# Tying a block's small copy behind its turned rows, an early all-ones matrix, and a sign moved into an eviction

## The chip, the cores and the metric

The kernel runs on one core of a Trainium2 chip. The metric is the device time of one execution in microseconds (us); lower is better. The engines are TensorE (PE in the rows, its weight loads PEld), VectorE (DVE), ScalarE (ACT), GpSimd (POOL) and SyncE (SP, which here only issues DMAs).

## The reference

The input x has 8 sequences of 2496 tokens with 256 channels. Each sequence is filtered along the tokens in the frequency domain; the 19968 filtered tokens then go through a mixture of eight experts, one expert for each token.

```
X = np.fft.rfft(x, axis=1)
y = np.fft.irfft(X * (filt_r + 1j * filt_i), n=S, axis=1)
...
logits = x @ w_gate + modality_bias[modality_id]
e_idx = np.argmax(logits, axis=1)
probs = np.exp(logits - max); probs /= probs.sum(-1)
...
h = np.maximum(x[mask] @ w1[e], 0.0)
out[mask] = gate_w[mask, None] * (h @ w2[e])
```

## The kernel before, in words

**Filter.** The transform of 2496 points is split into 48 x 52. Stage 1 (`stage1`, L194) multiplies by a 96x96 matrix and writes to a scratch tensor b1_d in DRAM. Stage 2 (`stage2`, L458) reads it back as tile `t` (L448), multiplies by `w2m` (L464), evicts `xf` (L477), multiplies by the filter tiles `g1` and `g2` on VectorE (L479, L480), multiplies by `a1m` and `a2m` into `pz` (L472, L473) and writes b2_d. Stage 3 (`stage3`, L491) reads b2_d, multiplies by `wbm`, and forms the gate's logits.

**Start-up.** The matrices are made on the chip in a part whose order is written out by hand (`manual_schedule`, L232 to L421). `a1m` and `a2m` come from transposing products with `perm`, evicted at L341: `a1m` on VectorE, `a2m` on ScalarE. The imaginary filter `g2` is loaded in two halves, of which the second is a copy of the first (L307, L308), and three VectorE instructions at L345 multiply it by a sign that depends on the partition alone (`sgn`). Much further on VectorE fills `ones_sq` (L376), with which a small matmul `mb_ps` (L409) spreads the gate's bias over the partitions. TensorE's `busy` matmuls (L824) have no use for the result; they are work put between the steps.

**Experts.** After a sequence's stage 3, `count` and `place` give each token a place in its expert's bin, and `scatter` (L596, an indirect DMA on the GpSimd queue, 20 for a sequence) writes the rows, each with its token number and gate, to `bins_d` in DRAM. `load` (L672) reads a block of 256 rows into tile `xs` (five buffers, L678, on the SP queue); it waits for the scatters that stand ahead of it in the program. `turn` (L688) copies the expert's weights (`w1`, L694), copies the token numbers and gates out of `xs` into `meta` (L700, eight buffers), transposes the rows on TensorE (`pT`, L704, one buffer) and copies the turned rows to `xT` (L705, VectorE). `up` (L710, matmuls `hps`, L715, eviction L720) needs `xT`; `down` (L722) makes `ops` (L728), scales it by the gate in `meta` into `osb` (L735) and writes the rows to the output with an indirect DMA on the GpSimd queue (`out_dram`, L737). A block takes 16 matmuls of each of L715 and L728; `down` of one block runs between the steps of `up` of the next. There are 79 blocks.

**Order.** Outside the part written by hand, a scheduler puts the instructions of each engine in order as the program is built; `tc.issue_after(x)` ties an instruction behind x. `behind` (L667) uses it for the weight copies and the loads. Nothing ties `meta`, whose only input is `xs`. On the chip each engine takes its instructions in that order.

Of the kernel before, what the change touches and what calls it, by code (L numbers as in the profile page):

```python
# [13 lines left out]
I32 = mybir.dt.int32  # L14
AF = mybir.ActivationFunctionType
# [5 lines left out]
P = 128  # L21
# [7 lines left out]
def kernel(  # L29
# [12 lines left out]
    nc = tc.nc  # L42
# [14 lines left out]
    NS = N1 // 2  # L57
    NTT = N2 // 2
    KA = 2 * N1
    KB = 2 * N2  # L60
# [10 lines left out]
    NI = BLK // P  # L71
# [4 lines left out]
    DW = D // 2  # L76
# [31 lines left out]
    a1m = fft_pool.tile([KB, NS, KB], BF16, name="a1m")  # L108
    a2m = fft_pool.tile([KB, NS, KB], BF16, name="a2m")
    g1 = fft_pool.tile([KB, NS, D], BF16, name="g1")  # L110
    g2 = fft_pool.tile([KB, NS, D], BF16, name="g2")
# [38 lines left out]
    def row_int(expr_ops, base, name):  # L150

        t = fft_pool.tile([P, 1], I, name=name + "_int")
        nc.vector.tensor_copy(t, base)
        for op, v in expr_ops:
            nc.vector.tensor_single_scalar(t, t, v, op=op)
        f = fft_pool.tile([P, 1], F32, name=name)
        nc.vector.tensor_copy(f, t)
        return f
# [3 lines left out]
    def col(name, fn):  # L162
        t = fft_pool.tile([P, 1], F32, name=name)
        fn(t)
        return t

    def ts(out, in_, s1, s2, op0=ALU.mult, op1=ALU.add):
        nc.vector.tensor_scalar(out, in_, scalar1=s1, scalar2=s2, op0=op0, op1=op1)
# [50 lines left out]
    ones_sq = const_pool.tile([P, P], F32)  # L219
# [12 lines left out]
    with tc.manual_schedule():  # L232
# [25 lines left out]
        nc.sync.dma_start(mb_sb, moe_modality_bias.rearrange("a e -> (a e)")[None, :])  # L258


        rows = row_int([], rows_i, "rows")
        bit0 = row_int([(ALU.bitwise_and, 1)], rows_i, "bit0")
        half = row_int([(ALU.arith_shift_right, 1)], rows_i, "half")
# [66 lines left out]
        sgn = col("sgn", lambda t: ts(t, x_hi, -2.0, 1.0))  # L330
        x_c0 = col("x_c0", lambda t: nc.vector.tensor_single_scalar(t, x_c, 0.0, op=ALU.is_equal))
        wt0 = col("wt0", lambda t: ts(t, x_c0, -0.5, 1.0))
        SPB = 4
        for s0 in range(0, NS, SPB):
            for src, dst in ((w2m, a1m), (w2x, a2m)):
                tp = pp.tile([P, EV * D], F32, tag="ps", name="tp")
                for i in range(SPB):
                    nc.tensor.matmul(tp[:KB, i * KB:(i + 1) * KB], lhsT=src[:, s0 + i, :], rhs=perm,
                                     start=True, stop=True)
                ev = nc.vector.tensor_copy if dst is a1m else nc.scalar.copy  # L340
                ev(dst[:, s0:s0 + SPB, :].rearrange("p s c -> p (s c)"), tp[:KB, 0:SPB * KB])  # L341
            if s0 == 0:
                nc.vector.tensor_scalar_mul(a1m[:, 0, :], a1m[:, 0, :], wt0[:KB])
        for ga, gb in ((1, 8), (8, 16), (16, NS)):
            nc.vector.tensor_scalar_mul(g2[:, ga:gb, :], g2[:, ga:gb, :], sgn[:KB])  # L345


        zs = col("zs", lambda t: nc.vector.tensor_single_scalar(t, quart, 0.0, op=ALU.is_equal))
# [24 lines left out]
        for b in range(3):  # L373
            mv = mrawc[:, b].rearrange("p g (t two) -> p g t two", two=2)
            nc.vector.tensor_copy(mids[KA:P, :, b:NYF:3], mv[KA:P, :, 3:4 * NYG:4, 0])
        nc.vector.memset(ones_sq, 1.0)  # L376

        eio_i = const_pool.tile([P, E], I32)
        nc.gpsimd.iota(eio_i, pattern=[[1, E]], base=0, channel_multiplier=0)
# [62 lines left out]
    ep = ctx.enter_context(tc.tile_pool(name="expert", bufs=2))  # L442
# [224 lines left out]
    def behind(what, n):  # L667

        m = marks[what]
        return tc.issue_after(m[-n]) if len(m) >= n else nullcontext()  # L670
# [17 lines left out]
    def turn(b):  # L688

        xh = b["xs"].bitcast(BF16)  # L690
        with behind("w1", 1):
            ej = nc.values_load(b["ej_i"], engines=(ET.DVE,), min_val=0, max_val=E - 1)
        b["w1"] = ep.tile([P, DC, F], BF16, tag="w1", name="w1")
        cp = nc.vector.tensor_copy(b["w1"].rearrange("p a f -> p (a f)"),  # L694
                              w1sb[:, ds(ej, 1)].rearrange("p o a f -> p (o a f)"))
        marks["w1"].append(cp.ins)
        b["xT"] = ep.tile([P, DC, NI, P], BF16, tag="xT", name="xT")

        b["meta"] = ep.tile([P, NI, 2], I32, tag="meta", bufs=8, name="meta")
        nc.vector.tensor_copy(b["meta"], b["xs"][:, :, DW:DW + 2])  # L700
        pT = op.tile([P, DC, NI, P], BF16, tag="tr")
        for dc in range(DC):
            for i in range(NI):
                nc.tensor.transpose(pT[:, dc, i, :], xh[:, i, dc * P:(dc + 1) * P], ident)  # L704
        nc.vector.tensor_copy(b["xT"], pT)  # L705
        b["hT"] = ep.tile([P, FT, NI * P], BF16, tag="hT", name="hT")

    FQ = 2
# [48 lines left out]
    class Experts:  # L757
# [26 lines left out]
        def begin(self, b):  # L784
            if b is not None:
                turn(b)
                self.fill()
# [144 lines left out]
```

## Time and profile before

| | us |
|---|---|
| median of 3 runs | 711.7 |
| lowest, highest | 709.67, 718.71 |
| profiled execution | 709.73 |
| its span, first to last instruction | 707.6 |
| TensorE busy in the span | 580.3 |
| VectorE, ScalarE, GpSimd busy | 369.9, 379.9, 365.8 |

The rows are of one profiled execution, 709.73 us, of which 2.1 us lie outside the span. Start times in rows count from the span's start. In rows of the timeline the bracket at the end is the idle time of the engine before the instruction, and what ended it. The span falls into a start-up (to about 180 us, when the first block of an expert is turned), a middle in which filter and experts are interleaved (to about 548 us), a stretch in which the last sequence's rows are scattered (to about 585 us), and an end in which only blocks are left.

### The profile page before, as it was taken

What the parts mean: (1) busy time and instruction counts of PE and PEld (TensorE: products, weight loads), DVE (VectorE), ACT (ScalarE), POOL (GpSimd) and SP (SyncE); (2) the same over time, 40 slices, a digit from 0 to 9 for tenths busy, and PEclk for the clock granted to TensorE, in tenths of its full rate; (3) what the DMA queues carried; (4) which work ended last, traced back from release to release, by engine and by line L of the source; (5) the groups of instructions that cost most, each with busy time, mean ns of one, the idle gap of its engine ahead of it and who ended that gap; (6) DMA issues with size and microseconds to landing.
All of it is one profiled execution on the core that took longest, in us unless ns stands there. A gap on an engine that the chain in (4) does not pass through costs nothing. (4 is left out here: it accounts for less than half of the span.)

```text
span 707.6 us, 16119 instructions
## 1 busy us (share of the span) xinstructions
PE 580.3 (82%) x4966; PEld 485.0 (69%) x4966; DVE 369.9 (52%) x1225; ACT 379.9 (54%) x672; POOL 365.8 (52%) x409
## 2 busy tenths in 40 slices
PE   3738678796997899898989979899869359999990
PEld 2527566565776688686878868687658249999990
DVE  8252134574655656564486557456446135555540
ACT  4414455564575577674767746454435126666660
POOL 8002111175376367376647727756766755555451
PEclk9969778898799699998999999899999799999996
DMA  9969889997767767656675565344223333333320
GB/s 154 227 132 201 178 226 210 224 244 180 187 177 176 188 165 184 191 132 179 161 194 151 160 168 136 116 112 137 91 89 107 103 104 102 106 113 101 97 76 20
DMA packets 84222, 106.08 MB, mean 150 GB/s; under 512 B 12164, under 2 KB 66250, under 8 KB 83980
## 3 DMA queue, kind: packets, MB, share of 16 engines
q0 software_dynamic: 21504, 50.75, 29.7%
q1 hardware_dynamic: 62632, 54.23, 29.1%
q8 instruction: 48, 0.79, 0.5%
q14 instruction: 38, 0.31, 0.1%
HBM read 71.07 MB, written 52.74 MB: 175 GB/s over the span
## 5 line engine op out<-in xcount | busy, mean ns | idle before, releaser
L720 ACT ACTIVATE hT<-hps 128x512 f16<-128x512 f32 x316 | 188.3, 597 | 174.6 <-PE hps L715 173.6
L715 PE MATMUL hps<-xT,w 128*128 128x256 f16 x1264 | 208.6, 286 | 33.5 <-DVE xT L705 33.2
L737 POOL DMA_INDIRECT out_dram<-osb,meta x158 | 158.5, 1003 | 126.6 <-DVE osb L735 73.1
L596 POOL DMA_INDIRECT bins_d<-yo,pos_i x160 | 162.1, 1013 | 77.9 <-issue 31.1
L728 PE MATMUL ops<-w2sb,hT 128*128 x1264 | 197.3, 279 | 0.3 <-issue 0.2
L715 PEld LDWEIGHTS <-w 128*128 128x128 f16 x1264 | 146.4, 148 | 45.8 <-DVE xT L705 36.1
L728 PEld LDWEIGHTS <-hT 128*128 128x128 f16 x1264 | 126.2, 100 | 15.7 <-issue 0.6
L700 DVE COPY meta<-xs 128x4 int32<-128x4 int32 x79 | 14.8, 188 | 120.5 <-DMA xs<-bins_d 110.6
L477 ACT CAST xf<-ps 104x512 f16<-104x512 f32 x96 | 56.2, 585 | 34.4 <-PE ps L464 32.2
L479 DVE TENSOR_TENSOR p<-xf,g 104x512 f16<-104x512 f16 x96 | 40.5, 422 | 63.8 <-ACT xf L477 63.4
L735 DVE TENSOR_SCALAR osb<-ops,meta 128x256 f32<-128x256 f32 x158 | 69.3, 475 | 5.5 <-PE ops L728 5.5
L694 DVE COPY w<-w1sb 128x2048 f16 x79 | 55.3, 700 | 28.5 <-PE hps L715 26.1
L486 ACT CAST z<-pz 104x512 f16<-104x512 f32 x96 | 56.6, 590 | 23.3 <-PE pz L473 12.5
L472 PE MATMUL pz<-p,a1m 104*104 104x256 f16 x192 | 52.2, 290 | 12.1 <-DVE p L479 4.1
L464 PE MATMUL ps<-t,w2m 104*104 104x256 f16 x192 | 41.1, 299 | 24.7 <-DMA t<-b_d 21.4
L473 PE MATMUL pz<-xf,a2m 104*104 104x256 f16 x192 | 51.0, 289 | 0.2 <-DVE xf L480 0.2
L824 PE MATMUL busy<-ident 128*128 128x256 f16 x296 | 50.9, 310 | 0.0
L205 ACT CAST t<-fp 96x512 f16<-96x512 f32 x57 | 32.3, 583 | 33.6 <-PE fp L200 19.8
L705 DVE COPY xT<-pT 128x512 f16<-128x512 f16 x79 | 33.1, 419 | 19.9 <-PE pT L704 19.5
L464 PEld LDWEIGHTS <-w2m 104*104 104x104 f16 x192 | 24.7, 139 | 26.4 <-issue 21.4
L533 DVE COPY yT<-lt 128x512 f16<-128x512 f16 x80 | 33.5, 419 | 17.0 <-PE lt L529 14.1
L480 DVE TENSOR_TENSOR xf<-xf,g 104x512 f16<-104x512 f16 x96 | 40.2, 419 | 2.2 <-DVE p L479 0.3
(194 smaller groups left out, 716.5 us busy)
## 6 DMA issues: line engine op xcount, KB each, us to landing
xs<-bins_d SPq DMA_DIRECT2D x79, 130.0 KB
t<-b_d SPq DMA_DIRECT2D x24, 416.0 KB
b_d<-z SPq DMA_DIRECT2D x48, 208.0 KB
xt<-in_x_dram POOLq DMA_DIRECT2D x24, 384.0 KB
b_d<-t SPq DMA_DIRECT2D x48, 192.0 KB
t<-b_d SPq DMA_DIRECT2D x24, 384.0 KB
w1sb<-in_moe_w_dram POOLq DMA_DIRECT2D x16, 256.0 KB
w2sb<-in_moe_w_dram POOLq DMA_DIRECT2D x8, 512.0 KB
```

What stands on the lines that cost most here:

```text
L464: mm = nc.tensor.matmul(ps[:KB, i, :], lhsT=w2m[:, s + i, :], rhs=st[g]["t2", s // SCH][:, s % SCH + i, :], start=True, stop=True)
L472: nc.tensor.matmul(pz[:KB, i, :], lhsT=a1m[:, s_ + i, :], rhs=p1[:, i, :], start=True, stop=False)
L473: nc.tensor.matmul(pz[:KB, i, :], lhsT=a2m[:, s_ + i, :], rhs=p2[:, i, :], start=False, stop=True)
L477: nc.scalar.copy(xf, ps[:KB])
L486: nc.scalar.copy(st[g]["z"][:, kk % 2], pz[:KB])
L596: ins = nc.gpsimd.indirect_dma_start(out=bins_d[:, :], out_offset=IOA(ap=st[g]["pos"][:rows, t:t + 1], axis=0), in_=st[g]["yw"][:rows, t, ...
L694: cp = nc.vector.tensor_copy(b["w1"].rearrange("p a f -> p (a f)"), w1sb[:, ds(ej, 1)].rearrange("p o a f -> p (o a f)"))
L715: mm = nc.tensor.matmul(hps[:, k, :], lhsT=b["w1"][:, dc, ft:F:FT], rhs=b["xT"][:, dc].rearrange("p i t -> p (i t)"), start=(dc == 0), sto ...
L720: nc.scalar.activation(b["hT"][:, q * FQ:(q + 1) * FQ, :], hps, AF.Relu)
L728: nc.tensor.matmul(b["ops"][:, i, :], lhsT=b["hT"][:, ft, i * P:(i + 1) * P], rhs=w2sb[:, ds(b["ej"], 1), ft, :], start=(ft == 0 and i == ...
L735: nc.vector.tensor_scalar_mul(osb[:, i, :], b["ops"][:, i, :], gate[:, i, :])
L737: ins = nc.gpsimd.indirect_dma_start(out=out[:, :], out_offset=IOA(ap=b["meta"][:, i, 0:1], axis=0), in_=osb[:, i, :], in_offset=None, bou ...
```

## The change

There are three edits. First, `ones_sq` is filled at the head of the part written by hand. Second, the three multiplications of `g2` by `sgn` go; the sign is applied while `a2m` is evicted on ScalarE (an activation that copies with a scale for each partition), except for its first slice of 104 columns, which is copied without it, so that the first of six evictions becomes two. Third, `meta` is copied after `xT` in the program, and `tc.issue_after` ties it behind the copy of the same block's turned rows.

```diff
+        nc.vector.memset(ones_sq, 1.0)
         rows = row_int([], rows_i, "rows")
...
-                ev = nc.vector.tensor_copy if dst is a1m else nc.scalar.copy
-                ev(dst[:, s0:s0 + SPB, :].rearrange("p s c -> p (s c)"), tp[:KB, 0:SPB * KB])
+                if dst is a1m:
+                    nc.vector.tensor_copy(dst[:, s0:s0 + SPB, :].rearrange("p s c -> p (s c)"),
+                                          tp[:KB, 0:SPB * KB])
+                    continue
+                a = 0
+                if s0 == 0:
+                    nc.scalar.copy(dst[:, 0, :], tp[:KB, 0:KB])
+                    a = 1
+                nc.scalar.activation(dst[:, s0 + a:s0 + SPB, :].rearrange("p s c -> p (s c)"),
+                                     tp[:KB, a * KB:SPB * KB], AF.Copy, scale=sgn[:KB])
...
-        for ga, gb in ((1, 8), (8, 16), (16, NS)):
-            nc.vector.tensor_scalar_mul(g2[:, ga:gb, :], g2[:, ga:gb, :], sgn[:KB])
...
-        nc.vector.memset(ones_sq, 1.0)
...
-        b["meta"] = ep.tile([P, NI, 2], I32, tag="meta", bufs=8, name="meta")
-        nc.vector.tensor_copy(b["meta"], b["xs"][:, :, DW:DW + 2])
         pT = op.tile([P, DC, NI, P], BF16, tag="tr")
         for dc in range(DC):
             for i in range(NI):
                 nc.tensor.transpose(pT[:, dc, i, :], xh[:, i, dc * P:(dc + 1) * P], ident)
-        nc.vector.tensor_copy(b["xT"], pT)
+        turned = nc.vector.tensor_copy(b["xT"], pT)
+        b["meta"] = ep.tile([P, NI, 2], I32, tag="meta", bufs=8, name="meta")
+        with tc.issue_after(turned.ins):
+            nc.vector.tensor_copy(b["meta"], b["xs"][:, :, DW:DW + 2])
```

The scheduler's order moves with it. The numbers behind names tell tiles apart; `meta` and `xT` of one block have numbers one apart in the kernel before (`meta_9399` belongs to `xT_9398`). On VectorE in the middle, shortly before the last sequence's rows are placed, the kernel before has:

```order
L692 ISA x2
L700 COPY meta_9301<-xs_8915 128x4
L700 COPY meta_9399<-xs_9047 128x4
L705 COPY xT_9027<-pT_9030 128x512
L533 COPY yT_9058<-lt_9049 128x512
L542 TENSOR_TENSOR lg_8324<-lg_8324,lt_9049 128x16
L700 COPY meta_9498<-xs_9159 128x4
L694 ISA
L694 COPY w1_9137<-w1sb_461 128x2048
```

The kernel after has at the same place:

```order
L698 ISA x2
L709 COPY xT_9025<-pT_9026 128x512
L712 COPY meta_9032<-xs_8662 128x4
L539 COPY yT_9056<-lt_9047 128x512
L548 TENSOR_TENSOR lg_8322<-lg_8322,lt_9047 128x16
L700 ISA
L700 COPY w1_9135<-w1sb_459 128x2048
```

Before, the turned rows of a block (`xT_9027`) stand behind the small copies of the blocks two and three later; after, ahead of every small copy but those of earlier blocks.

On VectorE while the last sequence's rows are scattered, before:

```order
L700 COPY meta_9597<-xs_9320 128x4
L705 COPY xT_9497<-pT_9500 128x512
L700 COPY meta_9696<-xs_9418 128x4
L694 ISA
L694 COPY w1_9594<-w1sb_461 128x2048
L735 TENSOR_SCALAR osb_9542<-ops_9459,meta_9301 128x256 x2
L692 TENSOR_LOAD ej_i_7080
L692 ISA x2
L700 COPY meta_9882<-xs_9517 128x4
L705 COPY xT_9596<-pT_9599 128x512
```

After:

```order
L709 COPY xT_9495<-pT_9496 128x512
L712 COPY meta_9502<-xs_9157 128x4
L700 ISA
L700 COPY w1_9592<-w1sb_459 128x2048
L742 TENSOR_SCALAR osb_9540<-ops_9457,meta_9305 128x256 x2
L698 TENSOR_LOAD ej_i_7078
L698 ISA x2
L709 COPY xT_9594<-pT_9595 128x512
L712 COPY meta_9601<-xs_9318 128x4
```

Before, `xT_9596` comes after the small copies of the next two blocks (`meta_9696`, `meta_9882`); after, its own small copy follows it.

On TensorE in the start-up, the end of stage 1 of the second sequence and the start of stage 2, before:

```order
L200 LDWEIGHTS w1m
L200 MATMUL fp<-xt,w1m 96x256
L200 LDWEIGHTS w1m
L200 MATMUL fp<-xt,w1m 96x256
L409 MATMUL mb_ps<-mb_sb,ones_sq 128x16
L464 LDWEIGHTS w2m
L464 MATMUL ps<-t_489,w2m 104x256
```

After:

```order
L339 LDWEIGHTS w2x
L339 MATMUL tp<-perm,w2x 104x104
L415 MATMUL mb_ps<-mb_sb,ones_sq 128x16
L470 LDWEIGHTS w2m
L470 MATMUL ps<-t_487,w2m 104x256
```

The bias matmul and stage 2 now follow the making of `a1m` and `a2m` at once; six pieces of stage 1 that stood ahead of them come later. The orders of GpSimd's and SP's DMAs in the middle and the end are almost the same in both kernels.

## Rows read from the trace of the kernel before

**Rows 1.** The page's first part: busy us, share of the span, instructions.

```profile
PE 580.3 (82%) x4966; PEld 485.0 (69%) x4966; DVE 369.9 (52%) x1225; ACT 379.9 (54%) x672; POOL 365.8 (52%) x409
```

**Rows 2.** Who waited for whom, whole span: us in total, times, longest.

```profile
DVE meta L700 <- DMA xs<-bins_d: 110.6, 41, 8.0
...
SPq L678 <- DMA bins_d<-yo,pos_i: 189.3, 54, 15.1
...
SPq L678 <- PE pT L704: 57.4, 26, 3.2
```

**Rows 3.** TensorE's waits from 177 to 548.5 us, same columns.

```profile
PE hps L715 <- DVE xT L705: 14.9, 6, 4.0
PE pz L472 <- DVE yo L539: 3.5, 1, 3.5
PE ps L464 <- DMA t<-b_d: 3.1, 1, 3.1
PE pT L704 <- DMA xs<-bins_d: 2.6, 2, 2.0
PE pz L472 <- DVE lg L542: 2.5, 1, 2.5
PE ps L464 <- DVE lg L542: 2.2, 1, 2.2
PE lt L524 <- DVE yo L539: 1.9, 1, 1.9
```

**Rows 4.** Timeline of VectorE, then TensorE, around 520 us: start, length.

```profile
508.71 0.20 DVE L700 COPY meta<-xs 128x4 int32<-128x4 int32 x1 [1.78 <-DMA xs<-bins_d]
...
526.08 0.17 DVE L700 COPY meta<-xs 128x4 int32<-128x4 int32 x1 [2.37 <-DMA xs<-bins_d]
526.16 0.42 DVE L705 COPY xT<-pT 128x512 f16<-128x512 f16 x1
...
520.27 0.39 PE L704 MATMUL pT<-ident,xs 128*128 128x128 f16 x4
...
526.63 0.77 PE L715 MATMUL hps<-xT,w 128*128 128x256 f16 x4 [3.87 <-DVE xT L705]
```

**Rows 5.** Stretches: length, busy of each engine, granted clock, DMA share, GB/s.

```profile
240.00:548.50 308.50, 281.84 (x2476) 232.28 (x2477) 183.48 (x636) 182.43 (x324) 192.03 (x195) 0.95 0.54 147
...
53.10:159.20 106.10, 84.00 (x679) 66.92 (x677) 45.21 (x146) 57.57 (x106) 28.20 (x42) 0.87 0.98 214
```

**Rows 6.** Timeline of VectorE, then TensorE, from 546 to 588 us.

```profile
559.44 0.17 DVE L700 COPY meta<-xs 128x4 int32<-128x4 int32 x1 [7.96 <-DMA xs<-bins_d]
559.52 0.42 DVE L705 COPY xT<-pT 128x512 f16<-128x512 f16 x1
...
577.05 0.17 DVE L700 COPY meta<-xs 128x4 int32<-128x4 int32 x1 [6.81 <-DMA xs<-bins_d]
...
546.97 0.38 PE L704 MATMUL pT<-ident,xs 128*128 128x128 f16 x4
...
560.00 1.07 PE L715 MATMUL hps<-xT,w 128*128 128x256 f16 x4 [10.89 <-DVE xT L705]
...
587.08 0.60 PE L715 MATMUL hps<-xT,w 128*128 128x256 f16 x4
```

**Rows 7.** Timeline of VectorE and TensorE in the start-up.

```profile
41.55 2.01 DVE L345 TENSOR_SCALAR g<-g,sgn 104x1792 f16<-104x1792 f16 x3 [11.92 <-DMA g<-g]
...
47.45 0.60 PE L409 MATMUL mb_ps<-mb_sb,ones_sq 1*128 1x16 f32 x2 [12.31 <-DVE ones_sq L376]
...
51.21 0.42 PE L473 MATMUL pz<-xf,a2m 104*104 104x256 f16 x1
```

**Rows 8.** DMA's busy share in tenths, 40 slices of 24 to 50 us.

```profile
DMA  9997989687577987999997966999971000000086
```

**Rows 9.** Groups of instructions: count, busy us, mean ns, idle before.

```profile
L479 DVE TENSOR_TENSOR p<-xf,g 104x512 f16<-104x512 f16 x96 | 40.5, 422 | 63.8 <-ACT xf L477 63.4
...
L341 ACT CAST a2m<-tp 104x416 f16<-104x416 f32 x6 | 3.0, 505 | 2.6 <-PE tp L338 2.6
```

## The prediction

> **What bounds the kernel now.** I read the page's shares first. TensorE is busy 82% of the span and no other engine over 54% [rows 1], so the time is TensorE's work plus its idle and its slow stretches, and the question is which idle goes away. The list of waits, sorted by length, has a strange second place: VectorE waited 110.6 us, 41 times, at the copy of `meta`, an instruction of 0.2 us, for the landing of `xs` [rows 2]. VectorE is not the bound, so this alone says nothing. It costs something only where TensorE waits for what stands behind that copy. The list of TensorE's own waits in the middle, 177 to 548.5 us, shows that it does: xT 14.9, yo 3.5 and 1.9, lg 2.5 and 2.2, together 25.0 us released by VectorE, against 2.6 us for `xs` itself and 3.1 us for the filter's loads [rows 3].
>
> The timeline of one such case gives the mechanism. A block's rows had landed by 508.71, where its own small copy ended its wait. TensorE transposed them at 520.27. Their copy to `xT` ran at 526.16, directly after a `meta` that had waited until 526.08, and TensorE stood idle 3.87 us for it [rows 4]. By the printed order that `meta` belongs to the block three later. So the rows that TensorE needed had been there for 11.6 us before their transposition, and VectorE waited for others. The last two long cases of the span have the same shape. At 546.97 TensorE transposed a block; the `meta` of the block two later held VectorE until 559.44; `xT` came at 559.52, and TensorE resumed at 560.00 after 10.89 us idle [rows 6].
>
> **The small copy behind the turned rows: the middle.** The edit adds and removes no instruction; 79 copies of under 0.5 us move back behind `xT`. `xT` waits for `pT` on TensorE, and `pT` for the block's own `xs`, so no VectorE instruction can be held any more by a load which TensorE itself does not need at that point. The stalls end by construction; how much of the 25.0 us comes back depends on what is late next. Next is TensorE at `pT`, waiting for `xs`. With a lead of 11.6 us in the case shown and only 2.6 us of such waits now, a few microseconds of TensorE's progress do not use it up. After that come the placing of a sequence and the filter's loads, which are not touched. I take 20 of 25.0; the ends are 10 (the leads shrink late in the middle, when GpSimd is the slower) and 25.
>
> The clock adds to this. From 240 to 548.5 us the mean granted clock was 0.95 [rows 5], and it has two levels, 2.4 and 1.2 GHz, so some 308.5 x 0.05 x 2 = 31 us passed at 1.2 GHz. That this follows idle stretches is seen in the scatter stretch: after the 10.89 us of idle a group of four L715 matmuls took 1.07 us, and later, with no idle ahead, 0.60 us [rows 6]. If all of the 31 us were busy, 15 us of work would be lost; part of it is the idle itself. I take 4, with ends 0 and 12.
>
> **The same, while the last sequence is scattered.** Here the blocks really arrive late. Loads wait for scatters (189.3 us of the SP queue's waiting in all [rows 2]), the scatters go at GpSimd's pace, and the edit does not hasten them. In the rows two small copies end their waits at 559.44 and 577.05 [rows 6]; a third stands between them. What changes is how far TensorE has got by then. Before, the block that lands at 577.05 begins its `up` at 587.08, because two earlier blocks are still to be done. After, TensorE has done them but for the part that stands behind this block's `pT` in its order, about half a block: some 2 us beside 577.05, so `up` at about 579.4. That is 7.7 us earlier, less 2 for a restart at 1.2 GHz after the idle that remains. I take 6, with ends 3 and 9. From there to the end TensorE is busy without a gap, so these microseconds reach the end of the span.
>
> **All-ones matrix and sign: the start-up.** Before, VectorE reached the sign multiplication and waited 11.92 us, until 41.55, for the second half of `g2`; `ones_sq` stood behind it, so the bias matmul waited 12.31 us, until 47.45, and stage 2 behind that; the first product with `a2m` ran at 51.21 [rows 7]. After, the fill is at the head, where it costs at most its own length, and the bias matmul passes. Stage 2 can start when `t` lands, but its product with `a2m` still needs `xf` times `g2`, so the copy at 41.55 is the new bound: two multiplies of 0.42 us [rows 9] give 42.4, which is 8.8 us before 51.21. The removed multiplications (2.01 us) lie inside that. On ScalarE six evictions of 505 ns [rows 9] become seven; one more is at most 0.5 us, hidden behind the wait for `t`.
>
> How much of 8.8 lasts is decided by DMA, which is full in what follows: its share is 0.98 from 53.1 to 159.2 us [rows 5]. Work can be brought forward only into the quiet part, the seven empty slices of 0.65 us and the one at a tenth before them, 24 + 30 x 0.65 = 43.5 to 48.7 us, 5.1 us in all [rows 8]. I take 4; the ends are 0 and 8.8.
>
> Weight loads on GpSimd's queue follow TensorE's progress, so they too move ahead, beside the copy of `g2` on SP's queue. The Trainium skill, "DMA: Bandwidth & Descriptors", section "Queues, rings and completion order", says that each DMA engine takes turns between the queues that have work, a packet at a time. By that the copy of `g2` could run at half pace from 35.1 us on (47.45 less 12.31) and land some 6 us later, and this term would be 2 or 3 in place of 4. No row here shows it, since GpSimd issued no weights while that copy ran.
>
> **The sum**, against the profiled execution of 709.7 us: 4 + 20 + 4 + 6 = 34, so 675.7. The median of the runs lies 2.0 us above the profiled one; taking half of that, **677 us**.
>
> **The rivals.** (a) The wait changes its name. If loads land later against TensorE's faster progress, TensorE waits at `pT` for `xs` as long as it now waits for `xT`; the middle gives nothing, and start-up and scatter stretch leave 709.7 - 10 = 700. For it: the SP queue waits 189.3 us for scatters, so the loads have a pace of their own. Against it: the lead of 11.6 us, and 2.6 us of waits at `pT` so far [rows 3].
>
> (b) Slower. `xs` has five buffers, and one is free only when `pT` and `meta` have read it. SP already waits 57.4 us, 26 times, for `pT` at that point [rows 2]; now it waits for `xT` (0.42 us) and `meta` (0.17) as well, some 0.7 us with the hand-overs, and the filter's stores and loads queued behind that load on SP wait too. This decides if loads land less than 0.7 us ahead of `pT`: then up to 79 x 0.7 = 55 us, so 709.7 - 34 + 55 = 731. The leads speak against it.
>
> (c) The edit does not act: something else holds VectorE at the same places, for instance `xT` itself, waiting for TensorE. Then only the start-up's 4 us remain: 706.
>
> **How the numbers follow.** Chances: forecast 0.84, (a) 0.09, (b) 0.04, (c) 0.03. The forecast's own ends are 661, most of the 25.0 and of the clock regained, and 693, with 10 in the middle, 3 in the scatter stretch and nearly nothing else. The range 661 to 695 leaves out (a), (b), (c) and a little at the fast end. About 2% is what a measurement here can tell from no change, so the line is at 697.5: faster 0.85, same 0.11, slower 0.04.
>
> **What would show it.** In the changed kernel the wait of `meta` for `xs` should all but vanish; TensorE's waits for `xT`, yo and lg from 177 us to the last placing should fall from 25 to about 5, with waits at `pT` for `xs` under 6 in that stretch; the clock there should come nearer 1. In the scatter stretch TensorE should stand at `pT`, not at `hps`. The product with `a2m` should come first at 42 to 48 us. If the waits at `pT` reach 20 us in the middle, I am wrong by (a); if SP's wait at the load grows by tens of microseconds, by (b).

## The result, and the profile after

The changed kernel takes 690.0 us (median of four runs, 686.2 to 695.4); the kernel before, beside it, 711.4. The ratio is 0.9686, with a 95% interval of 0.9592 to 0.9780. Measured again it was 0.9646 (0.9578 to 0.9714). The forecast was 677 us: the tied copy acted as described, and the gain was some 13 us smaller. The profiled execution took 686.2 us, 23.6 less than the one before. Some executions of every kernel are over 1.5% slower than its fastest; they count in the medians given in this document, but not in its ratios, which compare the means of the others, so that a ratio can differ from the quotient of its two medians by up to 0.7%.

The page's first part answers to [rows 1]: TensorE has the same busy time, and its share rises because the span shrinks by 23.2 us.

```profile
PE 580.6 (85%) x4966; PEld 486.7 (71%) x4966; DVE 371.6 (54%) x1222; ACT 380.3 (56%) x673; POOL 367.6 (54%) x409
```

The list of who waited for whom, whole span, of the changed kernel (microseconds in all, times, longest). It answers to [rows 2].

```profile
DVE xT L709 <- PE pT L708: 60.8, 57, 4.7
...
PE pT L708 <- DMA xs<-bins_d: 11.5, 4, 4.9
...
SPq L684 <- DMA bins_d<-yo,pos_i: 163.5, 51, 9.7
...
SPq L684 <- DVE meta L712: 52.7, 21, 3.2
```

The 110.6 us of `meta` waiting for `xs` are gone from the list. VectorE still waits 60.8 us at `xT`, now for TensorE, which costs TensorE nothing: an engine that waits for the one that bounds the kernel has time to spare. SyncE's wait for a free buffer is named after `meta` instead of `pT`, and is no longer than before (52.7 against 57.4); 52.3 us of it lie behind the last sequence's placing.

TensorE's own waits in the middle, 177 us to 534 us, answer to [rows 3].

```profile
PE ps L517 <- ACT t L205: 8.4, 2, 5.1
PE ps L470 <- DMA t<-b_d: 7.0, 2, 4.7
PE ps L517 <- DMA t<-b_d: 3.1, 1, 3.1
PE psO L578 <- DVE c L569: 2.0, 3, 0.9
PE pT L708 <- DMA xs<-bins_d: 1.9, 1, 1.9
PE hps L722 <- DVE xT L709: 0.3, 1, 0.3
PE lt L535 <- DVE lg L548: 0.3, 1, 0.3
```

The waits for xT, yo and lg, 25.0 us before, are 0.6. `pT` did not take their place (1.9 us). New at the head is 8.4 us, twice, for the eviction of stage 1 (`t`) on ScalarE, which itself waited for the store `b_d<-t`; these two are at 305 and 367 us.

To see where the time went I cut both spans at the same events: the cast of `pos_i` that ends a sequence's placing, for the second and for the last sequence. The columns are length, busy time of TensorE, weight loads, VectorE, ScalarE and GpSimd, granted clock, DMA share, GB/s. First the kernel before, then the changed one.

```profile
181.50:536.50 355.00, 321.63 (x2785) 262.17 (x2784) 212.70 (x742) 211.70 (x379) 218.53 (x223) 0.94 0.57 153
536.50:707.60 171.10, 135.21 (x1242) 123.85 (x1240) 72.78 (x189) 81.79 (x137) 89.96 (x92) 0.92 0.30 94
```

```profile
189.60:522.00 332.40, 312.73 (x2785) 257.65 (x2784) 217.20 (x739) 210.88 (x379) 220.76 (x223) 0.96 0.60 162
522.00:684.40 162.40, 135.70 (x1242) 124.40 (x1240) 71.74 (x192) 81.75 (x137) 90.14 (x93) 0.92 0.32 100
```

The middle holds the same 2785 matmul records and is 22.6 us shorter: TensorE's idle time falls from 33.4 to 19.7 us (355.00 - 321.63, 332.40 - 312.73), and its busy time by 8.9 us, with the granted clock at 0.96 instead of 0.94. The scatter stretch and the end are 8.7 us shorter. The start-up is 8.1 us longer (189.6 against 181.5). That adds up to -23.2. In the start-up TensorE's busy time grew by 8.7 us (580.6 - 312.73 - 135.70 = 132.2 against 580.3 - 321.63 - 135.21 = 123.5), so its 8.1 us are slower matmuls and not waits.

In the scatter stretch TensorE's timeline shows that it now stands at `pT`, as forecast, and no longer at `hps` as in [rows 6]. VectorE's rows behind it show `xT` waiting for `pT`, and the small copy behind `xT` without a wait. The loads themselves came no earlier: the three that TensorE waits for end those waits 23.1, 32.1 and 40.8 us behind the last placing at 522.0, and before, the small copies of [rows 6] ended theirs 22.9, 31.9 and 40.6 us behind 536.5.

```profile
545.05 0.61 PE L708 MATMUL pT<-ident,xs 128*128 128x128 f16 x4 [4.93 <-DMA xs<-bins_d]
554.06 0.60 PE L708 MATMUL pT<-ident,xs 128*128 128x128 f16 x4 [2.80 <-DMA xs<-bins_d]
562.75 0.40 PE L708 MATMUL pT<-ident,xs 128*128 128x128 f16 x4 [1.87 <-DMA xs<-bins_d]
...
563.18 0.42 DVE L709 COPY xT<-pT 128x512 f16<-128x512 f16 x1 [4.18 <-PE pT L708]
563.52 0.16 DVE L712 COPY meta<-xs 128x4 int32<-128x4 int32 x1
```

The start-up. In the kernel before, GpSimd issued the first weight load of the experts, and later TensorE waited for a load of stage 2, at:

```profile
47.68 1.11 POOL L435 DMA_DIRECT2D w1sb<-in_moe_w_dram  x2 [12.97 <-DVE eio L381]
...
134.60 0.59 PE L464 MATMUL ps<-t,w2m 104*104 104x256 f16 x2 [4.16 <-DMA t<-b_d]
```

The changed kernel, timeline of TensorE, VectorE and GpSimd, answers to this and to [rows 7]; the last line, DMA's share in 40 slices of 24 to 50 us, to [rows 8].

```profile
28.27 0.60 PE L415 MATMUL mb_ps<-mb_sb,ones_sq 1*128 1x16 f32 x2
...
44.30 0.27 PE L479 MATMUL pz<-xf,a2m 104*104 104x256 f16 x1 [1.12 <-DVE xf L486]
...
137.83 0.58 PE L470 MATMUL ps<-t,w2m 104*104 104x256 f16 x2 [7.85 <-DMA t<-b_d]
...
43.49 0.76 DVE L486 TENSOR_TENSOR xf<-xf,g 104x512 f16<-104x512 f16 x2 [6.87 <-DMA g<-g]
...
49.08 0.21 DVE L382 CAST mids<-mrawc 32x48 f16<-32x48 int32 x1
...
43.37 0.59 POOL L137 DMA_DIRECT2D xt<-in_x_dram  x1 [24.84 <-PE fp L200]
49.84 1.11 POOL L441 DMA_DIRECT2D w1sb<-in_moe_w_dram  x2 [5.88 <-DVE xf L486]
...
DMA  9998899852678887899988687699930569501740
```

The bias matmul is 19 us earlier, and the first product with `a2m` stands at 44.30, inside the forecast 42 to 48 and 6.9 us ahead of [rows 7]. But the first weight load went out at 49.84 us; before it was 47.68, and there too VectorE had released it, not TensorE. The weights' memory is that of a pool which is released behind the last cast of the modality numbers (`mids<-mrawc`): in each of the fourteen profiled runs this load goes out 0.5 to 0.7 us after that cast has ended. The casts now stand among the early products on VectorE, which wait for the copy of `g2`. That landed at 43.49 us here against 41.55 [rows 7]; in start_only, which has the same start-up, it landed at 41.02 and the weights went out at 47.62. So the edits leave the weights where they were, and the 2.2 us of this pair go with the landing of `g2`. DMA's quiet part is filled to less than half: the last ten slices, from 43.5 us, hold 3.7 tenths on average against 1.5 in [rows 8], and part of that is an input load which left at 34.12 us before and waits until 43.37 now, for input products that TensorE does behind stage 2.

### The profile page after: what moved, and what is told of

It is laid out like the page before. It is cut to its first block, busy times and chain, and to the rows that moved or that the text cites. A ratio compares the mean times of both kernels' runs of the same rounds, so it can differ in the third digit from the quotient of the medians.

```text
span 684.4 us, 16141 instructions
## 1 busy us (share of the span) xinstructions
PE 580.6 (85%) x4966; PEld 486.7 (71%) x4966; DVE 371.6 (54%) x1222; ACT 380.3 (56%) x673; POOL 367.6 (54%) x409
## 4 chain that ended last, share of the span: by engine, by line
PE 55%; DMA 21%; issue 9%; POOL 5%; DVE 5%; ACT 2%; SPq 0%; POOLq 0%; DVEq 0%; ACTq 0%
PE hps L722 15%; PE ops L735 12%; DMA b_d<-t 8%; DMA t<-b_d 7%; POOL out_dram L744 5%; PE ps L517 4%; PE ps L518 4%; PE busy L831 3%; PE lt L530 3%; PE pz L479 2%; PE ps L470 2%; PE pz L478 2%; PE pT L708 2%; DMA g<-g 2%; DMA bins_d<-yo,pos_i 2%
## 5 line engine op out<-in xcount | busy, mean ns | idle before, releaser
L744 POOL DMA_INDIRECT out_dram<-osb,meta x158 | 160.3, 1015 | 95.7 <-DVE osb L742 46.1
L485 DVE TENSOR_TENSOR p<-xf,g 104x512 f16<-104x512 f16 x96 | 40.6, 423 | 87.5 <-ACT xf L483 86.8
L470 PE MATMUL ps<-t,w2m 104*104 104x256 f16 x192 | 42.0, 306 | 32.1 <-DMA t<-b_d 25.9
L709 DVE COPY xT<-pT 128x512 f16<-128x512 f16 x79 | 33.4, 423 | 62.2 <-PE pT L708 60.8
L831 PE MATMUL busy<-ident 128*128 128x256 f16 x296 | 53.7, 321 | 0.0
L539 DVE COPY yT<-lt 128x512 f16<-128x512 f16 x80 | 33.8, 422 | 28.6 <-PE lt L535 23.0
L518 PEld LDWEIGHTS <-wbm 96*32 96x32 f16 x160 | 14.9, 93 | 44.6 <-issue 35.8
L517 PE MATMUL ps<-t,wbm 96*96 96x256 f16 x118 | 35.0, 297 | 12.7 <-ACT t L205 8.4
```

Source lines behind the costliest of these rows:

```text
L470: mm = nc.tensor.matmul(ps[:KB, i, :], lhsT=w2m[:, s + i, :], rhs=st[g]["t2", s // SCH][:, s % SCH + i, :], start=True, stop=True)
L517: nc.tensor.matmul(ps[:KA, i, :], lhsT=wbm, rhs=t4[:, t - t0, :], start=True, stop=True)
L744: ins = nc.gpsimd.indirect_dma_start(out=out[:, :], out_offset=IOA(ap=b["meta"][:, i, 0:1], axis=0), in_=osb[:, i, :], in_offset=None, bou ...
L831: mm = nc.tensor.matmul(t, lhsT=ident, rhs=ident[:, None, :].to_broadcast([P, NI, P]), start=True, stop=True)
```

## The experiments

Twelve kernels in four groups; each group ran on a chip of its own and shares its runs of the kernel before. All medians and ratios:

| kernel | median us | before beside it | ratio, 95% interval |
|---|---|---|---|
| meta_only | 687.6 | 718.3 | 0.9641, 0.9577 to 0.9705 |
| start_only | 718.4 | 718.3 | 0.9992, 0.9896 to 1.0089 |
| meta_sign | 686.7 | 718.3 | 0.9608, 0.9540 to 0.9676 |
| meta_ones | 691.9 | 718.3 | 0.9675, 0.9606 to 0.9744 |
| after_again | 689.7 | 717.0 | 0.9646, 0.9578 to 0.9714 |
| after_casts | 686.3 | 717.0 | 0.9574, 0.9483 to 0.9665 |
| meta_sign_b | 689.5 | 717.0 | 0.9577, 0.9497 to 0.9656 |
| no_copy | 682.6 | 717.0 | 0.9522, 0.9445 to 0.9599 |
| copy_act | 749.1 | 716.9 | 1.0443, 1.0339 to 1.0547 |
| no_wait | 774.1 | 716.9 | 1.0764, 1.0673 to 1.0854 |
| after_casts_b | 780.4 | 792.3 | 0.9828, 0.9769 to 0.9887 |
| casts_no_copy | 783.0 | 792.3 | 0.9885, 0.9828 to 0.9942 |

**meta_only: the tied copy alone.**

```diff
-        b["meta"] = ep.tile([P, NI, 2], I32, tag="meta", bufs=8, name="meta")
-        nc.vector.tensor_copy(b["meta"], b["xs"][:, :, DW:DW + 2])
...
-        nc.vector.tensor_copy(b["xT"], pT)
+        turned = nc.vector.tensor_copy(b["xT"], pT)
+        b["meta"] = ep.tile([P, NI, 2], I32, tag="meta", bufs=8, name="meta")
+        with tc.issue_after(turned.ins):
+            nc.vector.tensor_copy(b["meta"], b["xs"][:, :, DW:DW + 2])
```

> The kernel before with the copy of token numbers and gates tied behind the copy of the turned rows, and nothing else of the change. Theory (all of the gain is the copy's; the start-up edits lost about 8 us of it up to the second placing): 680 to 684 us, ratio 0.955 to 0.962, second placing again at 181 to 183 us after the start, 22 to 24 us gained between the second and the last placing and 8 us behind the last. Rival (the start-up edits gave their 4 us and the copy only 18): 692 to 695 us, ratio 0.972 to 0.978.

0.9641: as fast as the full change to within the intervals. The interval's upper end is below the rival's 0.972; the value itself lies a little above the theory's 0.962, which the interval covers. Its two stretches, cut at the same events:

```profile
184.70:520.90 336.20, 312.74 (x2785) 257.93 (x2784) 217.19 (x739) 210.75 (x379) 222.66 (x223) 0.95 0.60 161
520.90:686.00 165.10, 134.44 (x1242) 123.60 (x1239) 71.69 (x192) 81.79 (x137) 90.22 (x92) 0.92 0.32 98
```

18.8 us less in the middle and 6.0 behind the last placing, under the theory's sizes, and the second placing at 184.7 instead of 181 to 183. The measured gain of the change is in this edit; nothing of it needs the start-up.

**start_only: all-ones matrix first and the folded sign, the copy as before.** The edit is the start-up part of the change's diff, unaltered.

> The kernel before with the all-ones matrix first and the filter sign folded into the eviction; the copy of token numbers and gates as before. Theory (the lead of 6.9 us at the first product with a2m is given back by about 74 us, and the moved TensorE order costs something behind it): 711 to 719 us, ratio 1.000 to 1.011, second placing at 185 to 190 us against 181.5. Rival (the start-up edits give the 4 us of the prediction): 706 to 708 us, ratio 0.992 to 0.996, second placing at 176 to 179 us.

0.9992, so neither theory's size can be told apart from nothing: the interval is 7 us to either side. The stretches show that the start-up edits touch nothing later:

```profile
189.90:545.60 355.70, 321.52 (x2785) 261.91 (x2784) 212.04 (x741) 211.97 (x379) 218.77 (x223) 0.94 0.57 151
545.60:715.00 169.40, 134.17 (x1243) 122.95 (x1241) 72.64 (x189) 81.75 (x138) 89.97 (x92) 0.92 0.30 95
```

The middle is 355.7 us against 355.0 before and the rest 169.4 against 171.1, so the two halves of the change add up without touching each other. The second placing was at 189.9.

**meta_sign and meta_ones: one start-up edit each beside the tied copy.** The first leaves the fill of `ones_sq` where it was, the second leaves the sign multiplications.

Against the full change, meta_sign:

```diff
-        nc.vector.memset(ones_sq, 1.0)
         rows = row_int([], rows_i, "rows")
...
             nc.vector.tensor_copy(mids[KA:P, :, b:NYF:3], mv[KA:P, :, 3:4 * NYG:4, 0])
+        nc.vector.memset(ones_sq, 1.0)
```

and meta_ones, whose evictions of `a2m` are plain copies again:

```diff
+        for ga, gb in ((1, 8), (8, 16), (16, NS)):
+            nc.vector.tensor_scalar_mul(g2[:, ga:gb, :], g2[:, ga:gb, :], sgn[:KB])
```

> The tied copy and the folded sign, with the all-ones matrix set where it was before. TensorE's order at start-up is then that of the kernel before. Theory (what moved TensorE's order, and lost time, is the all-ones matrix alone; the folded sign only removes three multiplies of VectorE): the time of the kernel with the tied copy alone to within 2 us, 679 to 684 us, ratio 0.954 to 0.962. Rival (the folded sign is what loses or gains at start-up): the time of the full change, 688 to 692 us, ratio 0.967 to 0.972.

> The tied copy and the all-ones matrix first, with the sign multiplied into g2 on VectorE as before. TensorE's order at start-up is moved as in the full change. Theory: the loss of the full change or more, since the three sign multiplies now also stand ahead of the early products: 688 to 695 us, ratio 0.967 to 0.977. Rival (the moved order costs nothing): 680 to 684 us, as the tied copy alone.

Ratios of 0.9608 and 0.9675 with overlapping intervals: the order is the one the theory asked for, the difference is not shown. What the order of TensorE shows without any time: only the early all-ones matrix moves stage 2 ahead of the input pieces; with the sign alone the sequence at start-up is that of the kernel before. After these four I believed that the all-ones matrix costs 7 us, since the second placing stood at 189.6, 189.9 and 190.6 us with it and at 181.5, 184.7 and 182.9 without.

**after_again: the full change once more.**

> The full change once more, as the measure for the three kernels beside it. Every theory: ratio 0.964 to 0.974 to the kernel before; second placing at 189 to 191 us.

The ratio came as expected, the second placing did not: 184.4 us instead of 189 to 191. That took the belief down. Both executions of the same program, windows of 10 us from 130 to 160 us, first the profiled run of the result, then this one:

```profile
130.00:140.00 10.00, 2.17 (x11) 1.74 (x11) 2.12 (x8) 1.55 (x3) 0.86 (x2) 0.67 0.77 160
140.00:150.00 10.00, 10.00 (x46) 7.21 (x45) 7.42 (x39) 6.00 (x11) 3.88 (x6) 0.50 0.95 253
150.00:160.00 10.00, 10.00 (x56) 7.35 (x55) 3.39 (x13) 4.96 (x9) 7.30 (x9) 0.50 0.76 134
```

```profile
130.00:140.00 10.00, 2.99 (x15) 2.27 (x15) 2.82 (x10) 2.29 (x5) 1.57 (x3) 0.75 0.87 189
140.00:150.00 10.00, 9.93 (x76) 7.62 (x74) 8.17 (x44) 7.82 (x15) 4.21 (x5) 0.91 0.97 255
150.00:160.00 10.00, 7.76 (x73) 5.78 (x72) 5.48 (x17) 6.59 (x13) 8.14 (x9) 1.00 0.99 229
```

Up to 138 us they run alike: TensorE resumes at 137.83 in one and 137.17 in the other, after 7.85 and 7.01 us of waiting for `t`. Then one gets 0.50, which is 1.2 GHz, for 20 us, and the other 0.91 and 1.00: 102 matmuls against 149 from 140 to 160 us. There most of the 5 us between their second placings open (the first placings are at 144.7 and 143.8). So one profile's single start-up says nothing about a few microseconds here.

The middle took 333.1 us in this execution, close to 332.4 in the other, but the stretch behind the last placing took 170.7 instead of 162.4:

```profile
517.50:688.20 170.70, 136.55 (x1242) 124.69 (x1239) 71.27 (x192) 81.74 (x137) 92.75 (x95) 0.92 0.31 96
```

TensorE waited 16.3 us at `pT` there against 9.6, and the last of these waits ended 45.4 us behind the last placing instead of 40.8.

**after_casts: the full change, with the early products tied behind the casts.**

```diff
-            nc.vector.tensor_copy(mids[KA:P, :, b:NYF:3], mv[KA:P, :, 3:4 * NYG:4, 0])
+            cast = nc.vector.tensor_copy(mids[KA:P, :, b:NYF:3], mv[KA:P, :, 3:4 * NYG:4, 0])
...
-            nc.vector.tensor_mul(p1, xf, g1[:, sl, :])
+            with tc.issue_after(cast.ins) if (g, k) == (0, 0) else nullcontext():
+                nc.vector.tensor_mul(p1, xf, g1[:, sl, :])
```

> The full change, and the first multiply of stage 2 on VectorE tied behind the last cast of the modality numbers. Theory (the early products stood ahead of these casts on VectorE, the memory of the expert weights was therefore free later, and the weight loads and the input pieces behind them went out in one burst): the first weight load of the experts goes out at 44 to 47.5 us against 49.8, the second placing is back at 182 to 186 us, and the time is 3 to 7 us under that of the full change, ratio 0.957 to 0.965. Rival (the loss hangs on TensorE's own order, stage 2 ahead of the input pieces, and not on the casts): second placing still at 188 to 191 us, time as the full change to within 2 us.

The place of the theory holds. Timeline of VectorE, GpSimd and TensorE, and DMA's share from 24 to 50 us:

```profile
43.39 0.44 DVE L382 CAST mids<-mrawc 32x48 f16<-32x48 int32 x3
...
44.37 1.11 POOL L441 DMA_DIRECT2D w1sb<-in_moe_w_dram  x2 [2.57 <-DMA b_d<-t]
...
129.18 0.58 PE L470 MATMUL ps<-t,w2m 104*104 104x256 f16 x2 [5.36 <-DMA t<-b_d]
...
DMA  9998899649688888999878858996779209589999
```

The casts are done at 43.8, the weights go out at 44.37 instead of 49.84, DMA's last ten slices hold 6.9 tenths on average instead of 3.7, and the product that resumed at 137.83 in the full change (134.60 before) resumes at 129.18. One pair would not show a kept lead, since this point moves by a few microseconds with the execution; the profiled runs together do. In the six whose weights go out at 44.4 to 45.3 us (these casts ahead, or the early all-ones matrix left out with the sign folded) the product resumes at 127.2 to 135.0 us; in the seven at 47.6 to 51.0, with and without the start-up edits, at 134.6 to 139.2; no_wait, at 49.7, shows no such wait. What the lead is worth in the end is not shown: the clock was 0.50 and 0.58 from 130 to 150 us in this run, the second placing came at 181.8, no earlier than the 181.5 of the kernel before, and 0.9574 and 0.9646 have overlapping intervals.

**meta_sign_b: meta_sign once more, beside after_again.**

> The tied copy and the folded sign without the early all-ones matrix, on the same chip as the full change. Theory: second placing at 181 to 185 us and 3 to 8 us faster than the full change, ratio 0.956 to 0.965. Rival (the start-up edits make no difference that lasts): the same as the full change to within 2 us.

0.9577 against 0.9646: again on the theory's side, again not resolved. The second placing missed: 191.6 us instead of 181 to 185, and 8.7 later than in meta_sign, which is the same program.

**no_copy: no copy at all.** On top of meta_sign, the row numbers and gates are read from the block as loaded:

```diff
-        xs = ep.tile([P, NI, RW], I32, tag="xs", bufs=5)
+        xs = ep.tile([P, NI, RW], I32, tag="xs", bufs=6)
...
-        with tc.issue_after(turned.ins):
-            nc.vector.tensor_copy(b["meta"], b["xs"][:, :, DW:DW + 2])
...
-            gate = b["meta"][:, :, 1:2].bitcast(F32)
+            gate = b["xs"][:, :, DW + 1:DW + 2].bitcast(F32)
...
-                    out=out[:, :], out_offset=IOA(ap=b["meta"][:, i, 0:1], axis=0),
+                    out=out[:, :], out_offset=IOA(ap=b["xs"][:, i, DW:DW + 1], axis=0),
```

> As the tied copy with the folded sign, but without any copy: the gates and the token numbers are read from the block as it was loaded, which is then held until its rows are written out, in six buffers instead of five. Theory (a copy behind the turned rows is off the path, so that taking it away brings nothing): the time of the kernel with the tied copy to within 3 us, ratio 0.956 to 0.967. Rival (a block held longer keeps the SyncE queue waiting for a free buffer, and the loads land later): 700 to 715 us, ratio 0.98 to 1.00, with SyncE's load waiting over 100 us for the row writes and TensorE waiting over 20 us for blocks at pT.

0.9522, the best ratio of all and a little under the theory's 0.956, with an interval that reaches into it and overlaps that of meta_sign_b beside it. So taking the copy away brings what tying it brings, to within the spread: what cost time was where the copy stood. Its waits, same view, from an execution of 688.2 us:

```profile
SPq L684 <- DMA out_dram<-osb,xs: 132.5, 53, 7.0
SPq L684 <- DMA bins_d<-yo,pos_i: 114.5, 49, 6.3
...
PE pT L708 <- DMA xs<-bins_d: 15.8, 5, 5.6
```

This tests rival (b) of the prediction harder than the change itself could: SyncE's queue does wait 132.5 us for buffers to come free, with six of them, and still TensorE waits no longer for blocks than with a tied copy (15.8 us against 15.3 and 16.4 in meta_sign and meta_sign_b), and the kernel is no slower. Part of the wait only takes over what was waiting for scatters (114.5 us against 162.7 in meta_sign_b).

**copy_act: the untied copy on ScalarE.**

```diff
-        nc.vector.tensor_copy(b["meta"], b["xs"][:, :, DW:DW + 2])
+        nc.scalar.copy(b["meta"], b["xs"][:, :, DW:DW + 2])
```

> The kernel before with the copy of token numbers and gates on ScalarE, not tied; on that engine it stands some five blocks ahead of its block's own evictions. Theory (the copy costs by standing in an engine's order and waiting there for a block's load; the engine does not matter): VectorE's waits for blocks are gone, ScalarE waits over 110 us for them, TensorE waits for evictions of hps in place of xT, and the kernel is no faster than before: 711 to 745 us, ratio 1.00 to 1.04. Rival (what cost time was VectorE's own load, so that any engine with room would do): 680 to 692 us, ratio 0.955 to 0.972.

1.0443, a little over the theory's end, with 100.7 us of ScalarE's waiting for blocks where the theory had over 110. ScalarE's waits, then TensorE's:

```profile
ACT meta L700 <- DMA xs<-bins_d: 100.7, 44, 6.0
...
ACT meta L700 <- DMA out_dram<-osb,meta: 19.3, 12, 4.2
...
PE hps L715 <- ACT hT L720: 33.2, 20, 3.7
...
PE ps L511 <- ACT t L205: 14.2, 9, 3.5
```

The same wait moved with the copy, and TensorE waits for what ScalarE hands it: 33.2 us for evictions of `hps` against 0.2 before, 14.2 for `t` and 13.9 for `xf`, where before it waited 33.2 us for `xT`.

**no_wait: an untied copy of something that is always there.** The copy reads a table made at the start, so the rows go to other places and are not weighted:

```diff
-        nc.vector.tensor_copy(b["meta"], b["xs"][:, :, DW:DW + 2])
+        nc.vector.tensor_copy(b["meta"], fixed[:, min(len(turns), 78)])
```

> The kernel before with the copy untied and of the same form, but from a table in SBUF that is made at the start (token numbers in plain order, all gates one): the rows go to other places and are not weighted. The copy then has nothing to wait for, and stands in VectorE's order without a tie. Theory (only the copy's wait for its block's load cost time): 680 to 692 us, ratio 0.955 to 0.972, TensorE's waits for xT under 3 us in all. Rival (its place in the order or its own time cost): 705 to 715 us, ratio 0.99 to 1.005.

1.0764, missed by both. The edit did not take the wait away, it changed it. First TensorE's wait in the kernel before, whole span, then this run:

```profile
PE hps L715 <- DVE xT L705: 33.2, 9, 10.9
```

```profile
DVE meta L704 <- DMA out_dram<-osb,meta: 238.4, 66, 7.4
...
PE hps L720 <- DVE xT L710: 48.4, 27, 5.2
```

With nothing else to hold it, the copy was placed so far ahead that its own ring of eight buffers held it, until the rows of a block eight back were written out. The waits double (110.6 us before), and TensorE's waits for `xT` rise from 33.2 to 48.4 us. As a test of "the copy without a wait" it failed; as a second case of "a small instruction placed early that has to wait" it agrees. A copy that neither waits nor is tied was not tried; no_copy is the nearest to it.

**after_casts_b and casts_no_copy: is there a version that beats both?** The first repeats after_casts, the second adds the edits of no_copy to it.

> The full change with the first multiply tied behind the casts, once more: its ratio of 0.9574 stood beside 0.9646 of the full change, with intervals that overlap. Theory (the kept lead of 5 to 8 us at the products of stage 2 around 100 us is worth part of itself in the end): ratio 0.953 to 0.963 again, and the products of stage 2 at 98 us that stood at 104 in the full change. Rival (the granted clock between 130 and 170 us decides, and the lead is lost in its spread): the same 98 us, but a ratio of 0.964 to 0.972.

> All that looked best together: all-ones matrix first, folded sign, first multiply tied behind the casts, and no copy of token numbers and gates (read from the loaded block, six buffers). Theory (no copy and a tied copy are alike within the spread, and the kept lead is worth 3 to 6 us): ratio 0.950 to 0.960, 4 to 10 us under the full change. Rival (no copy is itself worth some us, as its median of 682.6 suggests): ratio 0.943 to 0.950.

All four ranges were missed. On the chip of this group the kernel before itself took 792.3 us, 11% more than in the others; the two kernels were 1.7% and 1.2% faster than it. The page of after_casts, then that of after_casts_b, the same program, say where it is not:

```profile
PE 576.1 (85%) x4966; PEld 484.2 (71%) x4966; DVE 370.5 (55%) x1222; ACT 379.9 (56%) x673; POOL 369.0 (54%) x409
```

```profile
PE 610.2 (78%) x4966; PEld 498.0 (64%) x4966; DVE 371.4 (48%) x1222; ACT 373.4 (48%) x673; POOL 364.8 (47%) x409
```

VectorE, ScalarE and GpSimd are as busy as ever, so no instruction of theirs was slower, and the start-up was not either (second placing at 184.8 us). From there to the last placing it took 405.0 us instead of 331.2, with TensorE's idle time spread over many places. Two kinds of wait stand out. The profile puts 33.8 us of ScalarE's waits and 24.4 us of VectorE's down to "remote", another core or a queue that it doesn't know, which no run outside this group has; and TensorE waits 29.6 us for nothing that the profile shows, against 0.7 in after_casts. What is behind them is open. The two kernels gained less there, and since neither has the tied copy alone, its own gain on that chip is not measured.

## Why the prediction was right, and where it was too high

**The middle: right.** "The stalls end by construction" is shown by the wait lists, by no_copy, and from the other side by copy_act and no_wait. Forecast 20 for the stalls and 4 for the clock, 24; measured 22.6 in the profiled pair, 21.9 in after_again and 18.8 in meta_only. The split was different. Of the 25.0 us of stalls 24.4 went, but 8.4 us of new waits for the eviction of `t` came (9.8 in after_again, 10.5 in meta_only), and some smaller ones, so that the idle time fell by 13.7 only. They come from the stores of stage 1, for which the sum had no term. The clock gave more: 8.9 us of busy time where I took 4. By the granted clock, 355.0 x 0.06 x 2 = 43 us passed at 1.2 GHz before and 332.4 x 0.04 x 2 = 27 us after, and half of the difference is 8 us. What is next in line after a stall should have been subtracted, and the faster matmuls behind fewer stalls added.

**The scatter stretch: right, with one exception.** Forecast 6, ends 3 and 9. From the last placing to the end the kernel before took 171.1 us and start_only 169.4. Seven of the eight profiled runs with a tied copy or none, outside the last group, took 162.4 to 168.0, which is 3.1 to 8.7 us less than 171.1; the profiled pair is the largest of these, meta_only has 6.0. The eighth, after_again, took 170.7, where the last block that TensorE waited for landed 4.6 us later than in the first execution of the same program. Why the gain is so little although `hps` waited 10.89 us before [rows 6] is what the timeline shows: the loads land when they did, and TensorE now waits for them at `pT`, 9.6 to 16.3 us in these runs, where it waited 18.6 for `xT`. In this stretch rival (a), the wait that changes its name, came in part.

**The start-up: wrong.** The step "Weight loads on GpSimd's queue follow TensorE's progress, so they too move ahead" failed. The first product came 6.9 us earlier, but the weight loads did not move ahead (49.84 us here and 47.62 in start_only, against 47.68), because their memory waits for casts which the early products had overtaken on VectorE. So the quiet part of DMA was filled to less than half, and where DMA is full the lead was gone: the product that waits for `t` came at 137.8, 137.2 and 134.9 us in the three executions of this start-up, and at 134.6, 137.9 and 139.2 with that of the kernel before. The bound "work can be brought forward only into the quiet part" was a sound one; that it would be filled was assumed. after_casts shows it: with the casts ahead again it is filled, and the product comes at 129.2 (131.7 and 127.2 in the last group). The term measured 0 (start_only, 7 us to either side) instead of 4. The 8.1 us by which the profiled run was behind at the second placing are not shown to be the edits': the same program came at 184.4 in another execution.

Whether the edits make the low clock at 130 to 160 us more likely is open. From the first to the second placing the kernel before, meta_only and copy_act took 39.8 to 40.9 us and no_wait 50.2; of ten profiled runs with a start-up edit one took 40.6 and nine 44.8 to 52.8. That points to it, from one or two executions of each program.

**The sum.** 34 us forecast; ratios of 0.9686 and 0.9646 take 22 and 25 us off 709.7. Of the missing 9 to 12 the start-up's term is 4, the middle's shortfall 1 to 5 and that of the scatter stretch up to 6, by the execution; the intervals reach 5 to 7 us to each side. The range had a slip: 10 in the middle and 3 in the scatter stretch leave 709.7 - 13 = 697, not 693, as its slow end. The 690.0 lie inside either way, nearer to the slow end than to the forecast's 677.

**The rivals.** (a) did not come in the middle: 1.9 us at `pT`. (b) did not: in the middle SyncE waited 0.3 us for `meta` at the load of `xs`, and no_copy held buffers far longer at no cost. (c) did not: VectorE does wait at `xT` for TensorE (60.8 us), but TensorE's waits for `xT` in the middle went from 14.9 us to 0.3.

The Trainium skill's rule on turns between queues ("DMA: Bandwidth & Descriptors", section "Queues, rings and completion order") had no case here: VectorE's wait for the copy of `g2` ended at 43.49 us instead of 41.55, with no weight load issued beside it. Over the runs that wait ended at 41.55 to 43.54 us without the start-up edits and at 41.02 to 43.49 with them, so the 1.9 us are within its spread, and no run shows the rule.

## What to carry to other kernels

In an engine that works in order, a tiny instruction that waits costs what the bound engine waits for behind it, not what it waits itself: here 33.2 us at `xT` and 10.1 at the filter's steps, where the copy waited 110.6. Look in the wait list for instructions that wait long for a load although they are needed late, and tie each behind the instruction that waits for the same load anyway; moving it to another engine moves the wait, and freeing it from one semaphore lets it run into the next.

Before counting on a lead at the start, follow every queue that has to move with it: here one memory pool, released behind a cast on VectorE, kept the weights back. And where the clock can drop by half for 20 us in one execution and not in the next, a few microseconds of one stage need more than one profile.

## What the runs showed of the hardware that I had not expected

The granted clock after a stop is not the same from run to run. Two executions of one program, with stops of 7.85 and 7.01 us that end within 0.7 us of one another, were granted 0.50 for the next 20 us in one and 0.91 and 1.00 in the other.

A chip on which the same program takes 11% longer (792.3 against 711 to 718 us) does not have to show it in any engine's busy time but TensorE's (610.2 us in after_casts_b against 576.1 in after_casts, for the same 4966 records); the start-up there was as fast as elsewhere (second placing at 184.8 us), and only what follows was longer. The waits for "remote" are its one mark in the profile that no other run has.
